# Opening of a linear-attention and feed-forward block: x tile 1 issued by ScalarE, w_phi and the block diagonals later, v of tile 0 evicted sooner, two q products ahead of phi_q@KV of tile 0

## The chip, the cores and the metric

The kernel runs on one core of a Trainium2 chip. The core has TensorE (PE, matmuls; its weight loads are shown as PEld), VectorE (DVE), ScalarE (ACT), GpSimd (POOL) and SyncE (SP), which run their own instructions in order and wait for each other through semaphores. DMA transfers are issued by an instruction on SP's or ACT's queue and move data between the chip's main memory and the core's own. The metric is the time of one execution on the device in microseconds (us). Several runs are timed, and the median counts; a separate execution is profiled and leaves the trace.

## The reference

One block over x of shape (1, 2048, 640) in bf16: layernorm, linear attention with a learned feature map (32 heads of 20), the output projection with a residual, a second layernorm, and a gated feed-forward part with a residual.

```python
h  = x + A(layernorm(x), wqkv, w_phi, wo)
h2 = h + (gelu(ln_h @ w_gate) * (ln_h @ w_up)) @ w_down      # ln_h = layernorm(h)

# A:
qkv = x @ wqkv                              # q, k, v: 32 heads of 20
pq, pk = q @ w_phi, k @ w_phi               # by head, 20x20
phi_q = concat(softmax(pq), softmax(-pq))   # 40 features by head
phi_k = concat(softmax(pk), softmax(-pk))
kv = phi_k.T @ v;  z = sum(phi_k over rows)
o  = (phi_q @ kv) / (phi_q @ z + 1e-6)
A  = o @ wo
```

## The kernel before

The 2048 rows are cut into 16 tiles of 128 rows (tile t holds rows p * 16 + t for p in 0..127), four tiles to a block x_sb[b]. The 640 columns are 5 chunks of 128. Every engine's instructions stand in the order in which the program writes them; no scheduler moves them.

The stages, in order:

- Opening (L186 to L503). SP issues the loads: x tiles 0 to 2, the v weights Wv in chunks (0, 1) and (2, 3), x tile 3, Wv chunk 4, x tiles 4 and 5 (L188 to L197), then five transposing loads of the k weights, WkT (L202). ACT issues the load of w_phi (L190) ahead of its table load. PE runs matmuls on constants (`warm`) until data is there.
- Tiles 0 and 1 are transposed without their scale: DVE takes the mean off (xc, L271 and L423), PE transposes (`tr_c`, L163), ACT copies the result out as LN1T (L164). Their rstd goes in later, when ACT takes v out of PSUM (`v_ev`, L315) and in the exponents. Tile 1's sums come from ACT (`st_act`, L406 and L408), with POOL's power behind it (L409 to L411).
- Tiles 2 and 3: DVE computes the statistics (`ln_stats`, L120 and L124), ACT the rstd as exp(-0.5 ln(var + eps)) (the function `root`, L130 and L131), DVE applies them (`ln_ap`, L155), PE transposes, DVE copies out (`ln_tp`). From tile 4 on POOL computes the rstd (L138, L139) and a DMA on SP transposes.
- `bd` (L432) builds the block diagonals BD of w_phi on DVE: w_phi, spread, times the mask hmask. `fold` (L247) multiplies WkT by BD on PE, which folds w_phi into the k weights: Wk2. It runs five times, and its results are taken out by ACT (L256, chunks 0, 1, 4) or DVE (L258).
- `v_part(t, c...)` (L311) is the part of v of tile t that the chunks c of the 640 rows of Wv give.
- PSUM is handed out in four buffers, taken in turn (`gtile`): a buffer is free again when its last reader is done.

Then the loop over 16 tiles (L509 on): k and its two exponents (ACT, L339), v of three tiles ahead, the sums by head and their reciprocals (DVE, L346 and L350), the division (L354, on POOL or DVE), and the products phi_k.T @ v (`kv_tile`, L373, into kvp). At its end come q products (`q_mm`, L395) with their exponents (`q_exp`, L400, ACT), and `kv_mask` (L380 and L382 on DVE) makes KV in two halves: one for the positive, one for the negative features.

Then phi_q @ KV of tile 0 (`attn_a(0, 1)`, L587): 40 small matmuls, the first 20 with the first half of KV, the other 20 with the second. Its result is copied out by ACT and DVE (L606). Around it stand q products: the group q has two column chunks of 128, each the sum of five matmuls of 128x512. What follows (the rest of attention, the feed-forward part) is not touched.

The semaphores of the DMAs that SP and ACT issue are eight, and are taken in turn; a DMA that takes one up again waits until the DMA that had it before has landed.

Of the kernel before, what the change touches and what calls it, by code (L numbers as in the profile page):

```python
# [17 lines left out]
def kernel(  # L18
# [12 lines left out]
    nc = tc.nc  # L31
    P = 128
# [7 lines left out]
    NC = D // P  # L40
# [31 lines left out]
    x_v = A_x.rearrange("b (p t) d -> p (b t) d", t=NT)  # L72
    o_v = out.rearrange("b (p t) d -> p (b t) d", t=NT)
    w_v = A_wqkv.rearrange("(c p) n -> p c n", p=P)
    phi_v = A_w_phi.rearrange("h d f -> (h d) f")
# [8 lines left out]
    x_sb = [const.tile([P, 4, D], BF16, name=f"x_sb{b}") for b in range(NB)]  # L84
    wphi = const.tile([P, NC, Dh], BF16, name="wphi")
# [24 lines left out]
    def gtile(name):  # L110
        return psG.tile([P, 2, 512], F32, name=name, tag="G")

    def ln_stats(pool, tiles, tag, act=True, between=None, log=False):

        n = len(tiles)
        mv = small(pool, [P, n, nc.vector.BN_AGGR_DIM], "mv" + tag)
        stats = small(pool, [P, n, 2, nc.vector.BN_STATS_DIM], "stats" + tag)
        for j, xt in enumerate(tiles):
            for i in range(2):
                nc.vector.bn_stats(stats[:, j, i, :], xt[:, i * HD:(i + 1) * HD])  # L120
                if between and i == j == 0:
                    between()
        for j in range(n):
            nc.vector.bn_aggr(mv[:, j, :], stats[:, j])  # L124
        ve = small(pool, [P, n], "ve" + tag)
        rstd = small(pool, [P, n], "rstd" + tag)
        if log is not False:

            def root():
                nc.scalar.activation(ve, mv[:, :, 1], ACTF.Ln, bias=eps)  # L130
                nc.scalar.activation(rstd, ve, ACTF.Exp, scale=-0.5)  # L131

            if log is True:
                root()
            else:
                log.append(root)
        else:
            nc.gpsimd.tensor_scalar_add(ve, mv[:, :, 1], EPS)  # L138
            nc.gpsimd.tensor_tensor(rstd, ve, nhalf[:, 0:n], op=ALU.pow)  # L139

        mr = small(pool, [P, n], "mr" + tag)
        if act:
            for j in range(n):
                nc.gpsimd.tensor_scalar(mr[:, j:j + 1], mv[:, j, 0:1], rstd[:, j:j + 1], -1.0,
                                        op0=ALU.mult, op1=ALU.mult)
        return [(xt, mv[:, j, 0:1], rstd[:, j:j + 1], mr[:, j:j + 1]) for j, xt in enumerate(tiles)]
# [11 lines left out]
    def transpose_to(dst, src, on_pe, on_dve=False):  # L158

        if on_pe:  # L160
            tp = psG.tile([P, 16, P], BF16, name="tp", tag="G")
            for c in range(NC):
                nc.tensor.transpose(tp[:, c, :], src[:, c * P:(c + 1) * P], ident)  # L163
            (nc.vector.tensor_copy if on_dve else nc.scalar.copy)(dst, tp[:, 0:NC, :])  # L164
        else:
            nc.sync.dma_start_transpose(dst, src)
# [19 lines left out]
    nc.gpsimd.memset(nhalf, -0.5)  # L186
    nc.gpsimd.memset(eps, EPS)
    nc.sync.dma_start(x_sb[0][:, 0:1, :], x_v[:, 0:1, :])  # L188
    nc.sync.dma_start(x_sb[0][:, 1:2, :], x_v[:, 1:2, :])
    nc.scalar.dma_start(wphi, phi_v.rearrange("(c p) f -> p c f", p=P))  # L190
    nc.scalar.add_instruction(mybir.InstLoadActFuncSet(name=nc.get_next_instruction_name(), act_func_set_id=6))
    nc.sync.dma_start(x_sb[0][:, 2:3, :], x_v[:, 2:3, :])
    nc.sync.dma_start(Wv[:, 0:2, :], w_v[:, 0:2, 2 * D:3 * D])
# [80 lines left out]
    def ln_st(*tiles, act=True, between=None, log=False):  # L274
        for t, v in zip(tiles, ln_stats(p1, [x_sb[t // 4][:, t % 4, :] for t in tiles], "1", act, between, log)):
            lnp[t] = v
# [8 lines left out]
    def ln_tp(t, on_dve=False):  # L285
        transpose_to(LN1T[t // 4][:, :, t % 4 * P:(t % 4 + 1) * P], lnp[t], True, on_dve)

    def lnT(t, c):
        b, tl = divmod(t, 4)
        return LN1T[b][:, c, tl * P:(tl + 1) * P]  # L290
# [14 lines left out]
    def v_part(t, *cs):  # L305

        if 0 in cs:
            pv[t] = gtile("pv")
        for c in cs:
            for u in range(2):  # L310
                nc.tensor.matmul(pv[t][:, u, 0:HD], lhsT=lnT(t, c), rhs=Wv[:, c, u * HD:(u + 1) * HD],  # L311
                                 start=(c == 0), stop=(c == NC - 1))

    def v_ev(t):
        nc.scalar.activation(vS[t % NV][:, :, 1:VC].rearrange("p (u h) f -> p u h f", u=2),  # L315
                             pv[t][:, :, 0:HD].rearrange("p u (h f) -> p u h f", f=Dh), ACTF.Copy,
                             scale=lnp[t][2] if t in CT else 1.0)
# [68 lines left out]
    def q_mm(j, part=(0, 1), kcs=range(NC)):  # L386

        if 0 in part and 0 in kcs:
            pqs[j] = gtile("pq")
        for i, bc in enumerate(QG[j]):  # L390
            if i not in part:
                continue
            b, c = divmod(bc, NC)
            for kc in kcs:
                nc.tensor.matmul(pqs[j][:, i, :], lhsT=Wq2[:, kc, c * P:(c + 1) * P], rhs=LN1T[b][:, kc, :],  # L395
                                 start=(kc == 0), stop=(kc == NC - 1))

    def q_exp(j, signs=(0, 1)):
        for s in signs:
            nc.scalar.activation(Eq[j][:, :, s, :], pqs[j][:, 0:len(QG[j])], ACTF.Exp, scale=(1.0, -1.0)[s])  # L400

    def st_act(t, i):

        xt, v = x_sb[0][:, t, :], va[t]
        if i == 0:
            nc.scalar.activation(sqa, xt, ACTF.Identity, scale=-1.0 / D, accum_out=v[:, 0:1])  # L406
        else:
            nc.scalar.activation(sqa, xt, ACTF.Square, bias=v[:, 0:1], accum_out=v[:, 1:2])  # L408
            nc.gpsimd.tensor_scalar(v[:, 2:3], v[:, 1:2], 1.0 / D, EPS, op0=ALU.mult, op1=ALU.add)  # L409
            nc.gpsimd.tensor_tensor(v[:, 3:4], v[:, 2:3], nhalf[:, 0:1], op=ALU.pow)  # L410
            nc.gpsimd.tensor_scalar(nrstd[t], v[:, 3:4], -1.0, None, op0=ALU.mult)  # L411
            lnp[t] = xt, None, v[:, 3:4], None
# [16 lines left out]
    def bd(c0, c1):  # L429

        n = c1 - c0
        nc.vector.tensor_tensor(BD[:, c0:c1], wphi[:, c0:c1, None, :].to_broadcast([P, n, 8, Dh]),  # L432
                                hmask[:, c0:c1, :, None].to_broadcast([P, n, 8, Dh]), ALU.mult)

    def tr_c(t):
        transpose_to(LN1T[0][:, :, t * P:(t + 1) * P], xc[t], True)
# [3 lines left out]
    xc.append(xc_a(1))  # L440
    tr_c(0)
    tr_c(1)
    ln_st(2, act=False, log=True)
    bd(0, NC)
    st_act(1, 1)
    warm(*[P] * 4)
    v_part(0, 0, 1)
# [2 lines left out]
    v_part(0, 2, 3)  # L450
    root = []
    ln_st(3, act=False, between=lambda: ln_tp(2, True), log=root)
    v_part(1, 2, 3)
    v_part(0, 4)
    root[0]()
    v_ev(0)
    v_part(1, 4)
    v_ev(1)
    v_part(2, *range(NC))
# [74 lines left out]
    q = len(QT)  # L534
# [67 lines left out]
    def attn_a(t, dve=0):  # L602
        attn_a_mm(t)
        AB, ab = ABs[t % 2], st[t, "ab"]
        for u in ((1, 0) if t in (4,) else (0, 1)):
            (nc.vector.tensor_copy if u >= 2 - dve else nc.scalar.copy)(  # L606
                AB[:, :, u * UH:(u + 1) * UH].rearrange("p s (r h) f -> p r s (h f)", r=2),
                ab[u][:, :, 0:2 * QH * KC].rearrange("p r (s x) -> p r s x", s=2))
        st[t] = AB
# [170 lines left out]


    q_mm(q, (0,))
    q_mm(q, (1,), (0, 1))
    attn_a(0, 1)
    q_mm(q, (1,), (2, 3, 4))
    q_exp(q)
    q_mm(q + 1)
    attn_b(0, True)
# [102 lines left out]
```

## Time and profile before

| | before |
|---|---|
| median of 3 runs | 273.13 us (273.03 to 273.55) |
| the profiled execution | 272.91 us, of which the span of instructions is 271.1 us |
| granted TensorE clock | 0.999 (mean of the span) |
| PE busy | 265.3 us (98%) |
| DVE busy | 175.1 us (65%) |
| ACT busy | 137.9 us (51%) |
| POOL busy | 100.7 us (37%) |
| DMA, first 6.8 us | 190 GB/s, 0.71 of the 16 engines' time |
| DMA, 6.8 to 13.4 us | 220 GB/s, 0.94 of the 16 engines' time |

Busy shares are means over stages with different limits, so they tell little of a single stage; the timelines do. In a timeline a line has the start in us from the span's beginning, the length in us, the engine, the line of the kernel, the operation, what it writes and reads, and how many instructions were merged. The bracket is the idle time of the engine just before, and what ended it. PEq, ACTq and SPq are the queues' own work, such as issuing a DMA. For the DMAs the page gives, by transfer, the median time from issue to landing: 3.3 us for an x tile of 160 KB (four of them), 4.4 us for two chunks of Wv (320 KB, twice) and for its last one (160 KB), 2.8 us for w_phi (25 KB).

### The profile page before, as it was taken

How to read it: one execution, taken by the hardware profiler on the slowest of the kernel's cores; microseconds unless marked ns; L12 is line 12 of the kernel's file. 1: busy time of each engine (PE TensorE's matmuls, PEld its weight loads, DVE VectorE, ACT ScalarE, POOL GpSimd, SP SyncE). 2: the span in 40 equal slices, each digit the busy share in tenths (PEclk: the TensorE clock that was granted, in tenths of full speed). 3: DMA queues.
4: the chain of work that ended last, by engine and by line, in shares of the span. 5: the costliest groups of instructions: out<-in, count | busy, mean ns of one | idle time of the engine just before them, and what ended most of it. 6: DMA issues, size and time to landing. Idle time of an engine off the chain costs nothing.

```text
span 271.1 us, 6984 instructions
## 1 busy us (share of the span) xinstructions
PE 265.3 (98%) x2843; PEld 170.7 (63%) x2862; DVE 175.1 (65%) x333; ACT 137.9 (51%) x238; POOL 100.7 (37%) x231
## 2 busy tenths in 40 slices
PE   7999999999999999999999999999999999999995
PEld 6777777764455887788755455774555576444574
DVE  5899999997877756694467783347768432333322
ACT  5769996887689675345524356114345600332100
POOL 5448889694002336384222564003165400000000
PEclk9999999999999999999999999999999999999999
DMA  7987357541787432232301222110122411000011
GB/s 189 221 201 171 53 98 89 57 104 52 232 271 223 150 99 59 69 73 51 73 4 51 48 48 51 48 52 0 51 48 48 52 48 51 24 0 0 2 48 48
DMA packets 45263, 22.10 MB, mean 81 GB/s; under 512 B 37808, under 2 KB 43184, under 8 KB 45232
## 3 DMA queue, kind: packets, MB, share of 16 engines
q1 hardware_dynamic: 44576, 21.64, 33.2%
q8 instruction: 22, 0.36, 0.5%
q10 hardware_dynamic: 656, 0.03, 0.2%
q14 instruction: 9, 0.07, 0.1%
HBM read 10.18 MB, written 2.62 MB: 47 GB/s over the span
## 4 chain that ended last, share of the span: by engine, by line
PE 85%; DVE 10%; DMA 2%; issue 1%; ACT 1%; SPq 0%; POOL 0%; DVEq 0%; POOLq 0%
PE gu L721 38%; PE pd L740 19%; PE po L661 8%; PE pq L395 7%; DVE sk L346 4%; PE pk L295 3%; DVE stats L120 3%; PE pv L295 3%; PE ab L587 2%; DMA Wv<-in_A_wqkv_dram 2%; PE kvp L373 1%; DVE rs L350 1%; PE wa L247 1%; DVE E L354 1%; PE pv L311 1%
## 5 line engine op out<-in xcount | busy, mean ns | idle before, releaser
L724 ACT ACTIVATE g<-gu 128x512 bf16<-128x512 f32 (+1 forms) x60 | 30.5, 510 | 63.4 <-PE gu L721 62.6
L727 DVE TENSOR_TENSOR GT<-gu,g 128x512 bf16<-128x512 f32 (+1 forms) x60 | 34.3, 578 | 43.9 <-PE gu L721 31.2
L721 PE MATMUL gu<-LN2T,Wg 128*128 128x512 bf16 (+1 forms) x287 | 61.2, 335 | 0.7
L721 PE MATMUL gu<-LN2T,Wu 128*128 128x512 bf16 (+1 forms) x300 | 61.8, 336 | 0.0
L740 PE MATMUL pd<-Wd,GT 128*128 128x320 bf16 (+2 forms) x396 | 53.5, 295 | 0.0
L740 PEld LDWEIGHTS <-GT 128*128 128x128 bf16 x396 | 37.9, 98 | 14.6 <-DVE GT L727 0.2
L721 PEld LDWEIGHTS <-Wu 128*128 128x128 bf16 x300 | 29.3, 98 | 22.6
L721 PEld LDWEIGHTS <-Wg 128*128 128x128 bf16 x300 | 28.6, 98 | 20.3
L295 PEld LDWEIGHTS <-LN1T 128*128 128x128 bf16 x290 | 27.9, 98 | 10.4
L743 DVE TENSOR_TENSOR y<-pd,x_sb 128x320 bf16<-128x320 f32 (+2 forms) x29 | 13.9, 479 | 29.5 <-PE pd L740 29.5
L354 POOL TENSOR_TENSOR E<-E,rs 128x640 bf16<-128x640 bf16 x24 | 30.2, 1288 | 6.5 <-DVE rs L350 2.6
L661 PE MATMUL po<-Wo,oT 128*128 128x320 bf16 x160 | 24.5, 299 | 0.0
L295 PE MATMUL pk<-Wk,LN1T 128*128 128x320 bf16 x160 | 24.4, 299 | 0.0
L395 PE MATMUL pq<-LN1T,Wq 128*128 128x512 bf16 x94 | 22.6, 379 | 0.3
L346 DVE TENSOR_REDUCE sk<-E 128x64 f32<-128x1280 bf16 x16 | 22.9, 1430 | 0.0
L400 ACT ACTIVATE Eq<-pq 128x1024 bf16<-128x1024 f32 (+1 forms) x26 | 19.9, 831 | 2.9 <-PE pq L395 2.7
L150 ACT ACTIVATE ln<-x_sb,v,rstd 128x640 bf16<-128x640 bf16 x14 | 12.9, 920 | 14.4 <-POOL v L700 14.3
L339 ACT ACTIVATE E<-pk 128x640 bf16<-128x640 f32 x28 | 18.7, 746 | 2.4 <-PE pk L295 1.8
L661 PEld LDWEIGHTS <-oT 128*128 128x128 bf16 x160 | 15.4, 98 | 6.9 <-ACT oT L164 0.2
L295 PE MATMUL pv<-Wv,LN1T 128*128 128x320 bf16 x130 | 19.8, 299 | 0.0
L636 DVE TENSOR_TENSOR tt<-AB,w 128x1280 bf16<-128x1280 f32 x12 | 17.8, 1486 | 1.0 <-POOL w L629 0.9
L616 POOL TENSOR_TENSOR pr<-AB 128x64 f32<-128x64 f32 x10 | 6.8, 677 | 26.7 <-DVE AB L597 20.6
(114 smaller groups left out, 289.6 us busy)
## 6 DMA issues: line engine op xcount, KB each, us to landing
out_dram<-y SPq DMA_DIRECT2D x15, 160.0 KB, 1.8
x_sb<-in_A_x_dram SPq DMA_DIRECT2D x6, 320.0 KB, 3.5
Wu<-in_B_w_up_dram SPq DMA_DIRECT2D x1, 1920.0 KB, 8.9
Wg<-in_B_w_gate_dram SPq DMA_DIRECT2D x2, 768.0 KB, 5.4
Wd<-in_B_w_down_dram SPq DMA_DIRECT2D x1, 1440.0 KB, 6.7
Wo<-in_A_wo_dram SPq DMA_DIRECT2D x1, 800.0 KB, 4.8
x_sb<-in_A_x_dram SPq DMA_DIRECT2D x4, 160.0 KB, 3.3
Wv<-in_A_wqkv_dram SPq DMA_DIRECT2D x2, 320.0 KB, 4.4
```

The costliest lines, as they stand in the source:

```text
L295: nc.tensor.matmul(ps[:, u, 0:HD], lhsT=lnT(t, c), rhs=W[:, c, u * HD:(u + 1) * HD], start=(c == 0), stop=(c == NC - 1))
L339: nc.scalar.activation(Ek[t][:, s, :].rearrange("p (u f) -> p u f", u=2), pk[:, :, 0:HD], ACTF.Exp, scale=((lnp[t][2], nrstd[t]) if t in C ...
L346: nc.vector.reduce_sum(sk, Ek[t].rearrange("p s (h f) -> p (s h) f", f=Dh), axis=AX.X)
L354: eng.tensor_tensor(e, e, rs[:, s * H:(s + 1) * H, None].to_broadcast([P, H, Dh]), ALU.mult)
L395: nc.tensor.matmul(pqs[j][:, i, :], lhsT=Wq2[:, kc, c * P:(c + 1) * P], rhs=LN1T[b][:, kc, :], start=(kc == 0), stop=(kc == NC - 1))
L400: nc.scalar.activation(Eq[j][:, :, s, :], pqs[j][:, 0:len(QG[j])], ACTF.Exp, scale=(1.0, -1.0)[s])
L636: nc.vector.tensor_tensor(tt.rearrange("p s (h f) -> p s h f", f=Dh), num, w[:, :, :, None].to_broadcast([P, 2, H, Dh]), ALU.mult)
L661: nc.tensor.matmul(pos[u], lhsT=st[t][:, c, :], rhs=Wo[:, c, u * HD:(u + 1) * HD], start=(c == 0), stop=(c == NC - 1))
L721: nc.tensor.matmul(gu[i][:, 0:n], lhsT=W[:, c, f * P:(f + 1) * P], rhs=LN2T[b][:, c, a0:a1], start=(c == 0), stop=(c == NC - 1))
L724: nc.scalar.activation(g[:, 0:n], gu[0][:, 0:n], ACTF.Gelu_apprx_tanh)
L727: nc.vector.tensor_tensor(st[b, "g", f][:, a0:a1], gu[1][:, 0:n], g[:, 0:n], ALU.mult)
L740: nc.tensor.matmul(ps, lhsT=st[b, "g", f][:, tl * P:(tl + 1) * P], rhs=Wd[:, f, f0:f1], start=(f == 0), stop=(f == NF - 1))
```

## The change

Four edits. The second load of x goes from SP's queue to ACT's, in w_phi's place. The load of w_phi goes on ACT behind the two copies of `tr_c`, and `bd` on DVE behind the statistics of tile 3. The last chunk of v of tile 0 goes ahead of chunks 2 and 3 of tile 1 on PE, and its eviction on ACT ahead of the rstd of tile 3. Of the five matmuls of the second chunk of the q group, four instead of two stand ahead of phi_q @ KV of tile 0.

```diff
     nc.sync.dma_start(x_sb[0][:, 0:1, :], x_v[:, 0:1, :])
-    nc.sync.dma_start(x_sb[0][:, 1:2, :], x_v[:, 1:2, :])
-    nc.scalar.dma_start(wphi, phi_v.rearrange("(c p) f -> p c f", p=P))
+    nc.scalar.dma_start(x_sb[0][:, 1:2, :], x_v[:, 1:2, :])
     nc.scalar.add_instruction(mybir.InstLoadActFuncSet(name=nc.get_next_instruction_name(), act_func_set_id=6))
...
     tr_c(0)
     tr_c(1)
+    nc.scalar.dma_start(wphi, phi_v.rearrange("(c p) f -> p c f", p=P))
     ln_st(2, act=False, log=True)
-    bd(0, NC)
     st_act(1, 1)
     warm(*[P] * 4)
     v_part(0, 0, 1)
...
     v_part(0, 2, 3)
     root = []
     ln_st(3, act=False, between=lambda: ln_tp(2, True), log=root)
+    bd(0, NC)
+    v_part(0, 4)
+    v_ev(0)
     v_part(1, 2, 3)
-    v_part(0, 4)
     root[0]()
-    v_ev(0)
     v_part(1, 4)
     v_ev(1)
...
     q_mm(q, (0,))
-    q_mm(q, (1,), (0, 1))
+    q_mm(q, (1,), (0, 1, 2, 3))
     attn_a(0, 1)
-    q_mm(q, (1,), (2, 3, 4))
+    q_mm(q, (1,), (4,))
     q_exp(q)
```

## The prediction

> **What bounds the kernel now.** I read the page's table of engines first (PE busy 265.3 of 271.1 us), then the timelines of PE, ScalarE (ACT) and VectorE (DVE) over the first 26 us, the issues of SP's queue, the busy time by windows to 41 us, and the timelines around KV (67 to 70 us). All times are us from the span's start.
>
> PE (start, length, engine, line, operation, in brackets the idle time before it):
>
> ```profile
> 0.83 3.89 PE L227 MATMUL wu<-const-bfloat16-1.0 128*128 128x512 bf16 x30 [0.83 <-PEq L875]
> 4.91 0.88 PE L163 MATMUL tp<-ident,xc 128*128 128x128 bf16 x10 [0.20 <-DVE xc L271]
> ...
> 6.49 1.79 PE L311 MATMUL pv<-Wv,LN1T 128*128 128x320 bf16 x12 [0.47 <-DMA Wv<-in_A_wqkv_dram]
> 8.12 0.44 PE L163 MATMUL tp<-ident,ln 128*128 128x128 bf16 x5
> ...
> 10.84 0.45 PE L163 MATMUL tp<-ident,ln 128*128 128x128 bf16 x5
> ```
>
> From 6.49 on PE runs without a pause that counts; the transposes of tiles 2 (8.12) and 3 (10.84) start as soon as their layernorm rows exist. So PE is full, but each of its opening steps stands on DVE and ACT. DVE:
>
> ```profile
> 6.67 0.94 DVE L432 TENSOR_TENSOR BD<-wphi,hmask 128x800 bf16<-128x800 bf16 x1
> 7.54 0.44 DVE L155 TENSOR_SCALAR ln<-x_sb,mv,rstd 128x640 bf16<-128x640 bf16 x1
> 7.89 0.48 DVE L120 BATCH_NORM_STATS2 stats<-x_sb 128x6 f32<-128x320 bf16 x1
> 8.60 0.49 DVE L164 COPY LN1T<-tp 128x640 bf16<-128x640 bf16 x1 [0.22 <-PE tp L163]
> 9.01 0.48 DVE L120 BATCH_NORM_STATS2 stats<-x_sb 128x6 f32<-128x320 bf16 x1
> 9.52 0.21 DVE L124 BATCH_NORM_AGGREGATE mv<-stats 128x2 f32<-128x12 f32 x1
> 9.65 0.44 DVE L120 BATCH_NORM_STATS2 stats<-x_sb 128x6 f32<-128x320 bf16 x1
> 10.33 0.45 DVE L155 TENSOR_SCALAR ln<-x_sb,mv,rstd 128x640 bf16<-128x640 bf16 x1 [0.24 <-ACT rstd L131]
> ```
>
> BD lies in a hole: without it DVE would stand until ACT's rstd of tile 2. The windows (length; busy time of PE, PEld, DVE, ACT, POOL) show what comes after:
>
> ```profile
> 20.00:27.00 7.00, 7.00 (x53) 5.03 (x52) 6.93 (x15) 6.92 (x11) 6.17 (x10) 1.00 0.80 174
> 27.00:34.00 7.00, 7.00 (x113) 5.01 (x111) 6.90 (x15) 7.00 (x12) 6.32 (x10) 1.00 0.32 56
> 34.00:41.00 7.00, 6.90 (x170) 5.02 (x168) 6.90 (x8) 7.00 (x12) 5.55 (x7) 1.00 0.49 91
> ```
>
> DVE is busy 20.73 of 21 us, so whatever it is late at 17 us it is late at 40. There PE meets it: DVE's E multiply (39.37, 1.29 long) ends at 40.66 and PE's phi_k product of tile 5 starts at about 40.7 behind it. So the opening is priced on DVE: a delay of ln of tile 3 arrives at 40.7 nearly whole, whatever PE gained.
>
> Issues and ACT in the opening:
>
> ```profile
> 0.79 0.46 ACTq L190 DMA_DIRECT2D wphi<-in_A_w_phi_dram  x1
> 1.28 1.28 ACT L191 ACT_TABLE_LOAD   x1 [1.28 <-PEq L875]
> ...
> 5.40 1.29 ACT L164 COPY LN1T<-tp 128x640 bf16<-128x640 bf16 x2
> 6.79 0.29 ACT L130 ACTIVATE ve<-mv,eps 128x1 f32<-128x1 f32 x1
> 7.11 0.20 ACT L131 ACTIVATE rstd<-ve 128x1 f32<-128x1 f32 x1
> ```
>
> ACT's next instruction starts only after its 0.46 of DMA issue.
>
> **Part 1: x tile 1 on ACT, w_phi later.** x tile 1 is issued at 0.79 instead of 1.26, and every later SP issue moves up one place of 0.46 to 0.51; the Wv chunk 4 issue goes from 3.69 to about 3.2. x tile 0 now shares its start with 160 KB of x tile 1 instead of 25 KB of w_phi; if it came up to 0.5 later, that would be hidden, for ACT, done with the copies at 6.69, waits until 7.6 (below). PE's 0.47 before the first pv can go (LN1T of tile 0, the first copy from 5.40, is there at 6.05), but PE then meets the transpose of tile 2 in order.
>
> The w_phi issue now stands on ACT behind the copies of tr_c and ahead of ve and rstd of tile 2. In the built programs' lists of waits the DMAs of SP and ACT take eight semaphores in turn (DMAHW0 to 7). In before, w_phi is among the first eight and waits for nothing. In after it is a later user of DMAHW6, and the instruction has a wait on DMAHW6 at 16, which is the complete landing of Wv chunk 4, the same count that the matmuls of v_part(0, 4) wait for. No data asks for that. That an issue stands in order behind its wait shows on SP: the issue of x tiles 8 and 9 (L474), which needs none of ln 4, starts at 14.14, after the transpose that waited from 12.01 to 12.89 for it. So behind w_phi on ACT wait: ve and rstd of tile 2 (for which DVE's ln 2 waits, and PE's transpose behind it), the square of tile 1, v_ev(0), the root of tile 3 and v_ev(1).
>
> Call W the landing of Wv chunk 4. Before: issue 3.69 plus 4.4 (its row of the issues) = 8.1. After: 3.2 + 4.4 = 7.6; or 8.1 less the 0.2% of the span, 0.5, that w_phi's queue took of the 16 engines, again 7.6. Bounds: above, 8.1 (no gain); below, 1,440 KB from x tile 0 to this chunk at 271 GB/s, the page's fastest slice, take 5.4, so 0.79 + 5.4 = 6.2, by when ACT is still in its copies (to 6.69). I take 7.6. The Trainium skill, page "DMA: Bandwidth & Descriptors", section "Issuing engines are not separate DMA queues", says that issuing from more engines only saves the issuers' own time, as all share 16 DMA engines. Were the two savings to add, W would be 7.1 and the time below half a microsecond less; by the rule, with the engines the limit, only w_phi's traffic counts.
>
> From W: wake 0.03, issue 0.46, gap 0.03, ve to the end of rstd 0.52 (6.79 to 7.31), to DVE 0.04: ln 2 starts at T = W + 1.08 = 8.68 instead of 7.54. If the issue runs under the copies instead, T is 7.35.
>
> **Part 2: BD after the mean of tile 3.** From ln 2 (T): ln 0.44, transpose on PE from T + 0.50, first matmul to DVE's copy 0.48 (8.12 to 8.60), copy at T + 0.98, stats +0.41, mean +0.51 (9.01 to 9.52), BD +0.13 at T + 2.03, stats of tile 4 +0.87 (6.67 to 7.54), ln 3 +0.42 at T + 3.32. ACT's rstd 3 is ready before that (mean ends T + 2.11, plus 0.60). Before, ln 3 was at 10.33. Its slip is T - 7.01 = W - 5.93 = 1.67; with no wait at all (T 7.35) still 0.34, for BD has left its hole.
> On PE: at the transpose of tile 2 it stands from about 7.7 to 9.2, then 18 matmuls of 0.136 to 11.9, then until tile 3's at 12.5. v_ev(0) sooner takes away the 0.28 for which fold(1) waited for a buffer until v_ev(1) was done (fold(0) ends at about 11.43, fold(1) starts at 11.71). PE's own slip is so about 1.4, DVE's 1.67, and at 40.7 the larger holds: +1.67.
>
> W_phi lands 2.8 after issue (its row): 7.63 + 2.8 = 10.43, BD wants it at 10.71: hidden, with 0.28 to spare. Bounds: 2.8, the same transfer early, and 4.4, Wv's under load; at 4.4 BD starts at 12.03, 1.3 later. I take 2.8, the same transfer on the same queue, and keep 4.4 for the range. The same page, section "Latency and other measured facts", gives 0.2 us for an HBM access and 2 us at high load; an estimate from it is up to 1.8 later, a slip of 3.2 in all; no row here shows it for this queue.
>
> **Part 3: two q products ahead.**
>
> ```profile
> 68.67 0.58 DVE L382 STREAM_TRANSPOSE KV<-KT 128x384 bf16<-128x384 bf16 x1
> ...
> 69.30 0.31 PE L587 MATMUL ab<-KV,Eq 32*128 32x44 bf16 x20 [0.27 <-DVE KV L382]
> ```
>
> PE does the first 20 products with KV (68.71 on), then stands for the second half of KV. Two 128x512 products of 0.216 go ahead: first half at 69.14, second at about 69.30 without a stop, and 0.43 less to do behind it. ACT's and DVE's work on ab (from 69.7) stays where it is; the next product with KV (72.45) waits for these copies, over by 70.7, so PE keeps the 0.43. Bounds 0.27 and 0.43; I take 0.43.
>
> **Sum.** +1.67 - 0.43 = +1.24 on the profiled execution of 272.91 (span 271.1, 1.8 around it), 274.15; the median, 273.13, is 0.22 above that execution: 274.4.
>
> **Rivals.**
> (a) ACT waits little, since Wv chunk 4 lands by about 6.6: slip 0.34 to 0.7, less 0.43: -0.1 to +0.3, some 273.2. For it: x tiles land in 3.3 by their row, 3.2 + 3.3 = 6.5. Against: they stood ahead of the 640 KB of Wv chunks 0 to 3.
> (b) w_phi late under the WkT transposes (DMA is 0.94 busy from 6.8 to 13.4): +1.3, 275.7. Against: its queue is its own.
> (c) Faster: w_phi's packets out of the way bring x tile 0 sooner than 3.30, by up to 0.5, and Wv by 6.2. Then T is 6.85, the slip -0.16, with 0.43 -0.6: 272.5. It decides only if both hold; against it, x tile 1 now runs beside x tile 0 in w_phi's place, with 160 KB for 25.
> (d) The change does not do what it says for PE's first wait: priced already, as PE's early start ends at the transpose of tile 2.
>
> **How the numbers follow.** The forecast 0.74, (a) 0.10, (b) 0.11, (c) 0.05; (d) is part of the forecast. Predicted 274.4. The forecast's own range: W 6.8 to 8.1 gives slips of 0.87 to 2.2, so 273.6 to 274.9. It is widened for (b) to 275.7 and towards (a) to 273.3. A measurement of this kernel tells apart about 0.2%, 0.55 us: faster is below 272.58, slower above 273.68. Faster 0.05 from (c); within: nearly all of (a) and the low edge of the forecast, 0.11; slower 0.84.
>
> **What would show it.** Right: on ACT, w_phi's issue at about 7.6, long after the copies, ve of tile 2 right behind; PE idle about 1.4 before the transpose of tile 2; ln 3 at about 12.0; PE after 40.7 about 1.7 late, after 70 about 1.2. Wrong: w_phi's issue before 6.7 (W early, or the issue does not stop ACT); BD waiting for w_phi's DMA (b); PE's delay gone by 41 us (DVE had slack after all); PE idle still before the second half of the products with KV.

## The result, and the profile after

| | before | after |
|---|---|---|
| median of 6 runs | 273.05 us (272.68 to 273.55) | 274.88 us (274.40 to 275.65) |
| ratio to before, 95% interval | | 1.0067 [1.0049, 1.0085] |
| span of the profiled execution | 271.1 us | 273.3 us |
| ln of tile 3 on DVE starts | 10.33 us | 12.96 us |
| first product of phi_q@KV of tile 0 on PE | 68.71 us | 71.74 us |

The change made the kernel slower by 1.83 us at the median, 2.2 us between the spans of the two profiled executions. The loss is made in the first 13 us, where the layernorm of tile 3 comes 2.63 late; the q products give some 0.4 back. In the runs of one kernel of the experiments, e2, three of the six executions had a granted clock of 0.994 and took 276.5 to 276.6 us; in all others here the clock was 0.998 or more.

The changed kernel has one source line less ahead of the helpers, so L310 is L311 of before, L431 is L432. ScalarE's (ACT's) timeline of the changed kernel:

```profile
5.80 1.29 ACT L164 COPY LN1T<-tp 128x640 bf16<-128x640 bf16 x2 [0.34 <-PE tp L163]
...
8.13 0.39 ACTq L442 DMA_DIRECT2D wphi<-in_A_w_phi_dram  x1
8.57 0.29 ACT L130 ACTIVATE ve<-mv,eps 128x1 f32<-128x1 f32 x1 [1.49 <-DMA Wv<-in_A_wqkv_dram]
8.90 0.20 ACT L131 ACTIVATE rstd<-ve 128x1 f32<-128x1 f32 x1
```

The copies end at 7.09. Then ACT stands until Wv chunk 4 has landed, issues w_phi at 8.13, and only then comes to the rstd of tile 2. The bracket names the releaser: a transfer of Wv, which neither w_phi nor the rstd reads. The trace's records of the issues also name the semaphores. Eight numbers occur among the DMAs of SP and ACT, and w_phi's issue waits on 109, the one that the issue of Wv chunk 4 at 3.20 had taken; its count was full at 8.11. DVE:

```profile
9.13 0.45 DVE L155 TENSOR_SCALAR ln<-x_sb,mv,rstd 128x640 bf16<-128x640 bf16 x1 [2.55 <-ACT rstd L131]
...
11.05 0.21 DVE L124 BATCH_NORM_AGGREGATE mv<-stats 128x2 f32<-128x12 f32 x1
11.65 0.99 DVE L431 TENSOR_TENSOR BD<-wphi,hmask 128x800 bf16<-128x800 bf16 x1 [0.39 <-DMA wphi<-in_A_w_phi_dram]
12.56 0.49 DVE L120 BATCH_NORM_STATS2 stats<-x_sb 128x6 f32<-128x320 bf16 x1
12.96 0.43 DVE L155 TENSOR_SCALAR ln<-x_sb,mv,rstd 128x640 bf16<-128x640 bf16 x1
```

DVE stands 2.55 for that rstd, then 0.39 more for w_phi itself. PE behind it:

```profile
6.54 1.85 PE L310 MATMUL pv<-Wv,LN1T 128*128 128x320 bf16 x12 [0.26 <-ACT LN1T L164]
9.64 0.45 PE L163 MATMUL tp<-ident,ln 128*128 128x128 bf16 x5 [1.24 <-DVE ln L155]
...
13.45 0.45 PE L163 MATMUL tp<-ident,ln 128*128 128x128 bf16 x5 [0.92 <-DVE ln L155]
```

PE's first pv starts no sooner than before (6.54 against 6.49), and the transposes of tiles 2 and 3 each wait for DVE's ln. The chain of work that ended last, in order of time (start, length, what), shows the way in one piece:

```profile
3.20 4.91 DMA Wv<-in_A_wqkv_dram
8.11 0.02 issue
8.13 3.42 DMA wphi<-in_A_w_phi_dram
...
11.65 0.09 DVE BD L431
...
13.05 0.36 DVE ln L155
```

Two transfers stand in series there, though no data passes between them. The page's issues have the same two (KB each, us from issue to landing), after and, in the second fence, before:

```profile
Wv<-in_A_wqkv_dram SPq DMA_DIRECT2D x1, 160.0 KB, 4.9
...
wphi<-in_A_w_phi_dram ACTq DMA_DIRECT2D x1, 25.0 KB, 3.4
```

```profile
Wv<-in_A_wqkv_dram SPq DMA_DIRECT2D x1, 160.0 KB, 4.4
...
wphi<-in_A_w_phi_dram ACTq DMA_DIRECT2D x1, 25.0 KB, 2.8
```

Last, DVE's E multiply for which PE waits at the end of the first long stretch, before and (second fence) after, and PE's products with KV, likewise:

```profile
39.37 1.29 DVE L354 TENSOR_TENSOR E<-E,rs 128x640 bf16<-128x640 bf16 x1
```

```profile
41.96 1.29 DVE L353 TENSOR_TENSOR E<-E,rs 128x640 bf16<-128x640 bf16 x1
```

```profile
68.71 0.32 PE L587 MATMUL ab<-KV,Eq 32*128 32x44 bf16 x20
```

```profile
71.74 0.47 PE L587 MATMUL ab<-KV,Eq 32*128 32x44 bf16 x40
```

The multiply is 2.59 late: of ln 3's 2.63 nothing that counts was absorbed in 29 us. The products with KV, two groups of 20 with an idle 0.27 between them before, now run as one group of 40.

### The profile page after: what moved, and what is told of

It reads as the page before. It is cut to its first block, busy times and chain, and to the rows that moved or that the text cites. A ratio compares the mean times of both kernels' runs of the same rounds, so it can differ in the third digit from the quotient of the medians.

```text
span 273.3 us, 7002 instructions
## 1 busy us (share of the span) xinstructions
PE 266.3 (97%) x2862; PEld 170.1 (62%) x2862; DVE 174.8 (64%) x333; ACT 138.2 (51%) x238; POOL 101.8 (37%) x231
## 4 chain that ended last, share of the span: by engine, by line
PE 94%; DMA 3%; SPq 1%; issue 0%; DVE 0%; DVEq 0%
PE gu L721 38%; PE pd L740 19%; PE pq L394 8%; PE po L661 8%; PE pk L294 8%; PE pv L294 7%; PE ab L587 2%; DMA Wv<-in_A_wqkv_dram 2%; PE kvp L372 2%; DMA wphi<-in_A_w_phi_dram 1%; PE wa L246 1%; PE tp L163 0%; DVE stats L120 0%; SPq L193 0%; SPq L194 0%
```

## The experiments

Eight kernels in two groups of four. Each ratio is against the kernel before, run on the same chip in the same group (medians of before: 273.24 us in the first, 273.37 us in the second).

| run | ratio to before, 95% | ratio less 1, times the median of before | ln of tile 3 | Wv chunk 4 lands |
|---|---|---|---|---|
| e1 w_phi at the front | 1.0018 [1.0004, 1.0032] | +0.5 us | 11.26 | 8.1 |
| e2 w_phi behind the rstd | 1.0089 [1.0063, 1.0115] | +2.4 us | 12.91 | 8.2 |
| e3 q products alone | 0.9984 [0.9970, 0.9998] | -0.4 us | 10.27 | 8.1 |
| e4 x tile 1 on ACT alone | 1.0029 [1.0010, 1.0048] | +0.8 us | 10.57 | 8.1 |
| e5 BD late alone | 1.0019 [1.0006, 1.0033] | +0.5 us | 10.78 | 8.0 |
| e6 v of tile 0 sooner alone | 1.0000 [0.9989, 1.0011] | 0.0 us | 10.65 | 8.5 |
| e7 v sooner and q products | 0.9980 [0.9972, 0.9989] | -0.5 us | 10.21 | 8.3 |
| e9 the wait alone | 1.0042 [1.0030, 1.0055] | +1.1 us | 12.69 | 8.2 |

The last two columns are from each run's one profiled execution; where they differ by a tenth or two they tell nothing. The landing is the issue plus the time of its row.

**e1: the changed kernel with w_phi back at the front.** Theory A is the prediction's: ACT waits for Wv chunk 4, and w_phi then comes late. Theories B and C are the rivals that could carry the loss without it.

```diff
+    nc.scalar.dma_start(wphi, phi_v.rearrange("(c p) f -> p c f", p=P))   # behind x tile 1
...
     tr_c(1)
-    nc.scalar.dma_start(wphi, phi_v.rearrange("(c p) f -> p c f", p=P))
```

> The changed kernel, but w_phi is issued by ScalarE right behind x tile 1, at the start. Theory A (ScalarE waits for Wv chunk 4 ahead of the rstd of tile 2, and w_phi then comes late): both are gone, ve of tile 2 stands right behind the copies at about 7.2, ln of tile 3 at about 11.1 (10.33 before, 12.96 in the changed kernel), the time about 273.4. Theory B (x tile 1 beside x tile 0 makes tile 0 late, 0.4 in the profile) and theory C (BD out of its hole on DVE, 0.34): if these carry most of the loss, ln of tile 3 stays near 12.5 and the time at 274.3 or more.

273.64 us. ACT goes on from the copies at once, and ln 3 starts at 11.26:

```profile
6.02 1.29 ACT L164 COPY LN1T<-tp 128x640 bf16<-128x640 bf16 x2 [0.34 <-PE tp L163]
7.19 0.31 ACT L130 ACTIVATE ve<-mv,eps 128x1 f32<-128x1 f32 x1
```

With this one line at the front the loss falls from 1.83 to some 0.5. Theory A holds for most of the loss; B and C together would be worth what is left, plus the 0.4 that the q products give back. Alone (e4 and e5 below) they add up to 1.3 instead of 0.9, which the intervals leave room for.

**e2: w_phi one step later.** The wait stays, but behind the rstd.

```diff
     tr_c(1)
-    nc.scalar.dma_start(wphi, phi_v.rearrange("(c p) f -> p c f", p=P))
     ln_st(2, act=False, log=True)
+    nc.scalar.dma_start(wphi, phi_v.rearrange("(c p) f -> p c f", p=P))
```

> The changed kernel, but w_phi is issued one step later, behind the rstd of tile 2 on ScalarE, so that the wait for Wv chunk 4 no longer holds up that rstd. If ScalarE's wait alone costs the time: ln of tile 2 at about 7.8 instead of 9.13, ln of tile 3 at about 11.2, time about 273.5. If the late landing of w_phi is a second path of the same length (issued at about 8.1, landing 3.4 later): PE's 1.24 before the transpose of tile 2 goes, but BD still starts at about 11.6, ln of tile 3 stays at about 12.9 and the time at about 274.8.

275.84 us, or 274.82 to 275.20 without the three executions named above, against 274.40 to 275.65 of the changed kernel: nothing gained. DVE's ln 2 starts at 7.73, and PE does the transpose of tile 2 at 8.42 without a stop, but:

```profile
11.60 0.99 DVE L431 TENSOR_TENSOR BD<-wphi,hmask 128x800 bf16<-128x800 bf16 x1 [1.56 <-DMA wphi<-in_A_w_phi_dram]
12.51 0.49 DVE L120 BATCH_NORM_STATS2 stats<-x_sb 128x6 f32<-128x320 bf16 x1
12.91 0.43 DVE L155 TENSOR_SCALAR ln<-x_sb,mv,rstd 128x640 bf16<-128x640 bf16 x1
```

So the same wait acts on two paths of nearly one length, by the rstd and by w_phi's own landing. To take away one leaves the other.

**e9: the wait without the late w_phi.** e1, and in the place of the late load a second load of w_phi into a tile that nothing reads; it takes the same semaphore as Wv chunk 4.

```diff
     tr_c(1)
+    nc.scalar.dma_start(wphj, phi_v.rearrange("(c p) f -> p c f", p=P))
```

> The changed kernel with w_phi loaded early (as in the run with w_phi at the front), and in the place where it was issued a second load of w_phi into a tile that nothing reads. That second load takes the semaphore of Wv chunk 4 and waits for it, so ScalarE's wait is there and w_phi is not late. Theory A: ScalarE's wait alone makes ln of tile 2 start at about 9.2 and ln of tile 3 at about 12.5 (12.96 in the changed kernel, 11.26 with w_phi at the front): time about 274.7. If the wait cost nothing by itself: 273.6, as with w_phi at the front.

274.61 us. The DMA issue at 8.23 and what it does to ACT are as in the changed kernel, and BD follows the mean of tile 3 with no wait:

```profile
8.23 0.37 ACTq L444 DMA_DIRECT2D wphj<-in_A_w_phi_dram  x1
8.66 0.29 ACT L131 ACTIVATE ve<-mv,eps 128x1 f32<-128x1 f32 x1 [1.31 <-DMA Wv<-in_A_wqkv_dram]
```

```profile
11.27 1.09 DVE L433 TENSOR_TENSOR BD<-wphi,hmask 128x800 bf16<-128x800 bf16 x1
...
12.69 0.42 DVE L156 TENSOR_SCALAR ln<-x_sb,mv,rstd 128x640 bf16<-128x640 bf16 x1
```

The wait alone puts ln 3 1.43 later than in e1 and costs 0.0024 of the time by the difference of the two ratios, some 0.7 us, where 1.1 was expected; the two intervals leave room for both. In the profiles the E multiplies are 0.78 apart (40.90 in e1, 41.68 here), for in e1's DVE stood 0.55 for x tiles 6 and 7 on the way (last section).

**e4: x tile 1 on ACT alone**, w_phi right behind it on the kernel before.

```diff
-    nc.sync.dma_start(x_sb[0][:, 1:2, :], x_v[:, 1:2, :])
+    nc.scalar.dma_start(x_sb[0][:, 1:2, :], x_v[:, 1:2, :])
     nc.scalar.dma_start(wphi, phi_v.rearrange("(c p) f -> p c f", p=P))
```

> The kernel before with x tile 1 issued by ScalarE at the start and w_phi right behind it, nothing else. Theory B: x tile 0 lands about 0.4 later (3.7 instead of 3.3), nothing of it is regained, ln of tile 3 at about 10.7, time 273.4. Rival (the loads of Wv come sooner and PE starts sooner): ln of tile 3 at 10.3 or before, time 273.0 or less.

273.77 us, slower. DVE's first statistics wait longer for x tile 0 than before. Before, and in the second fence e4:

```profile
3.30 0.89 DVE L120 BATCH_NORM_STATS2 statsc<-x_sb 128x6 f32<-128x320 bf16 x2 [0.96 <-DMA x_sb<-in_A_x_dram]
```

```profile
3.82 0.89 DVE L120 BATCH_NORM_STATS2 statsc<-x_sb 128x6 f32<-128x320 bf16 x2 [1.48 <-DMA x_sb<-in_A_x_dram]
```

The two tiles run beside each other, and the one that heads every chain lands half a microsecond later. PE's first pv starts at 6.67, no sooner than before. The rival falls. That nothing of the delay is regained did not come: of the 0.52, 0.24 is left at ln 3 (10.57) and 0.36 at the E multiply (39.73). The profiled execution, 273.26, is among the quickest of the ten (273.19 to 275.14), so no trace shows where the slower ones lose the rest of the 0.8.

**e5: BD late alone** (w_phi early) and **e6: v of tile 0 sooner alone**, each on the kernel before. e5, and in the second fence e6:

```diff
     ln_st(2, act=False, log=True)
-    bd(0, NC)
...
     ln_st(3, act=False, between=lambda: ln_tp(2, True), log=root)
+    bd(0, NC)
```

```diff
     ln_st(3, act=False, between=lambda: ln_tp(2, True), log=root)
+    v_part(0, 4)
+    v_ev(0)
     v_part(1, 2, 3)
-    v_part(0, 4)
     root[0]()
-    v_ev(0)
```

> The kernel before with BD on DVE behind the mean of tile 3, nothing else (w_phi is there early). Prediction's part 2 without the wait: BD leaves the hole in which DVE stood for the rstd of tile 2, ln of tile 3 slips by 0.34 from 10.33 to about 10.7, the time by as much, 273.5. Rival (the hole is no hole, or DVE has slack until 40 us): ln of tile 3 slips by up to 0.9, or the time does not move: 273.1.

273.77 us, ln 3 at 10.78: 0.45 late, where 0.34 was expected. BD's old place was nearly free, its new one is not. The working put the transpose of tile 2 on PE 0.50 behind ln 2; here PE was still at its first pv, and it came 0.73 behind (7.25 and 7.98).

> The kernel before with the last chunk of v of tile 0 and its eviction sooner, nothing else. If the stretch to 40.7 is set by DVE: PE's 0.28 before fold(1) goes, and PE waits that much longer for DVE later: no change, 273.1. Rival (PE sets it): 272.8.

273.25 us, no change, as expected, but not for the reason expected. The stop of 0.28 before fold(1) is gone, and yet PE's next v product starts 1.26 behind fold(0), as before. Before, and in the second fence e6:

```profile
11.13 1.38 PE L247 MATMUL wa<-BD,WkT 128*128 128x140 bf16 x18
12.39 1.52 PE L295 MATMUL pv<-Wv,LN1T 128*128 128x320 bf16 x10
```

```profile
11.44 1.22 PE L247 MATMUL wa<-BD,WkT 128*128 128x140 bf16 x18
12.70 1.52 PE L295 MATMUL pv<-Wv,LN1T 128*128 128x320 bf16 x10
```

In both traces that v product starts some 0.05 after ACT's copy of fold(0) has ended (11.64 + 0.69 before, 11.96 + 0.69 in e6); that it waits for this buffer is a reading of these times. PE gained nothing there that it could give back to DVE at 41 us, so this run does not test whether PE or DVE sets the stretch.

**e3: the q products alone, e7: with v of tile 0 sooner.**

```diff
     q_mm(q, (0,))
-    q_mm(q, (1,), (0, 1))
+    q_mm(q, (1,), (0, 1, 2, 3))
     attn_a(0, 1)
-    q_mm(q, (1,), (2, 3, 4))
+    q_mm(q, (1,), (4,))
```

> The kernel before with the two q products ahead of phi_q@KV of tile 0 alone. Prediction's part 3: PE's 0.27 to 0.43 ahead of the second half of KV goes and is kept to the end: 0.43 less, 272.6. Rival: the time is taken back later, by the copies of the products with KV or by a buffer: 273.05.

272.88 us: 0.44 less by the ratio, the wait for KV is gone and stays gone.

> The kernel before with v of tile 0 sooner and the two q products ahead, without the moved loads and without BD's move: the part of the change that costs nothing. Expected 272.7 to 272.8, 0.4 below before; if v of tile 0 also counts, 272.5.

272.94 us, 0.55 less by the ratio: faster than both kernels. Its interval and that of e3 overlap, so only the q products are shown to be worth keeping.

## Why the prediction was right, point by point

In short: ACT's wait and its way into the time came as forecast. A second path, w_phi's own late landing, came on top, and the wait itself was longer than taken.

- **The bound.** Right: DVE carries a delay to 40.7 us whole. Ln 3 late by 2.63, 2.58, 2.36 and 0.45 (after, e2, e9, e5) makes the E multiply late by 2.59, 2.54, 2.31 and 0.41. e7 shows it for a delay of DVE alone: PE reaches the transpose of tile 3 no later than before (10.72 against 10.84), DVE then stands 0.60 for a load of x (last section), the E multiply is 0.55 late (39.92), and the span grows by 0.2 though the q products take 0.4 off. What PE's own slip would have cost without DVE's is not shown: in the changed kernel its transpose of tile 3 is late by 2.61 too (13.45 against 10.84).
- **PE's 0.28 before fold(1).** A misreading, at no cost to the sum, which went by DVE's slip. From fold(0) to the next v product PE takes 1.26 before, in the changed kernel (13.74 to 15.00) and in e6 alike.
- **The wait on DMAHW6.** Right in place and kind: ACT stopped ahead of the rstd of tile 2 until Wv chunk 4 had landed. The semaphore is the one of Wv chunk 4 in the trace too. e1 (no wait) and e9 (the wait alone) show that it costs.
- **The size of W.** One of the two terms that were mis-sized by half a microsecond: 7.6 predicted, 8.11 measured, the upper bound. The issue did come 0.49 earlier (3.20), but the landing took 4.9 instead of 4.4. In e1, e2, e4 and e9 too the earlier issue brought no earlier landing (8.1 to 8.2). The floor of 6.2 was none: 271 GB/s is the mean of a slice of 6.8 us, and the trace before has 370 GB/s from 6.5 to 7.5. The rule of the Trainium skill that was weighed, from "DMA: Bandwidth & Descriptors", section "Issuing engines are not separate DMA queues", speaks of this: issuing from several engines only saves the time that the issues take. The trace agrees, and goes further, for w_phi's traffic out of the way brought nothing either.
- **From W to ln 2.** 1.08 predicted, 1.02 measured (8.11 to 9.13).
- **w_phi's landing.** The other mis-sized term, and one that the prediction had named as a sign of being wrong: hidden with 0.28 to spare, by 2.8 from issue to landing; it took 3.42, and DVE waited 0.39. That is rival (b), at a third of its price. With the gap before it this puts BD at 11.65, 2.52 after ln 2 instead of the 2.03 of the working. e2 shows that this path alone is as long as the wait's: ln 3 at 12.91, against 12.69 with the wait alone (e9).
- **BD out of its hole.** 0.34 predicted, 0.45 measured in e5.
- **The sum.** ln 3's slip: 1.67 predicted, 2.63 measured; 0.5 of the difference is W, 0.5 is BD's later start, and the 1.02 takes 0.06 off. Less 0.43: 2.2 between the profiled spans, and 1.83 between the medians, against 1.24. That 274.88 lies inside the forecast's own range (to 274.9) is in part luck: by the two profiled executions, 272.91 and 275.01, the change costs 2.1, and 273.13 + 2.1 lies above it, in the part that was widened for (b).
- **x tile 0 beside x tile 1.** Predicted: up to 0.5 late, and hidden behind the wait. Both hold: 3.70 instead of 3.30 after, and alone, in e4, with no wait to hide behind, the kernel is 0.8 slower (0.3 to 1.3), of which the trace shows 0.36.
- **The q products.** 0.43 predicted; 0.44 in e3, with an interval of 0.05 to 0.8.
- **Rivals (a) and (c)** needed Wv chunk 4 by 6.6 or 6.2. No profile had it before 8.0.

## What to carry to other kernels

A DMA that is moved to a later place in the program may take up a semaphore that another transfer still holds, and its issue then waits, with all that stands behind it on its engine, for a transfer that it has nothing to do with; look at the waits of the built program, not at the data. Work moved out of a hole in a full engine costs time in its new place: 0.45 of BD's 0.95 in e5. A stop that an edit removes is a gain only if the next step of that engine does not stand behind something else; in e6 it did, and of the four edits only the one past the first long stretch, the q products, is shown to pay.

## What the runs showed of the hardware

- With x tile 1 issued by ACT beside x tile 0, the first statistics started at 3.70 to 3.96 in five profiles (after, e1, e2, e4, e9), against 3.28 to 3.36 in the five with x tile 1 on SP: a second x tile started at the same moment made the first one later.
- The same w_phi transfer of 25 KB took 2.8 to 2.9 from issue to landing at the start (before, e3, e5, e6, e7), 3.6 to 3.7 right behind x tile 1 on ACT's queue (e1, e4, e9), and 3.3 to 3.5 beside the transposing loads WkT (after, e2, the second load of e9).
- The wait for a semaphore shows a second time: in e1, e4 and e9 the issue of x tiles 4 and 5 is the ninth, takes up x tile 1's semaphore, and starts at 4.12, 4.04 and 4.14, 0.01 to 0.02 after x tile 1 has landed; in after, where it is the eighth, it starts at 3.68.
- The landing of x tiles 6 and 7 moves between executions: in e1's profile DVE stood 0.55 for it, between the opening and the E multiply, in e7's 0.60, in e3's 0.24, in those of before and after not at all. From e1:

```profile
16.89 0.89 DVE L120 BATCH_NORM_STATS2 stats<-x_sb 128x6 f32<-128x320 bf16 x2 [0.55 <-DMA x_sb<-in_A_x_dram]
```

The E multiply in e1 was so 1.53 late (40.90) though ln 3 was only 0.93 late. A single profile is good for a chain, but not for a tenth of a microsecond of it.
